# k^T v of the last attention unit ahead of its scores, and the first batch's remainder transposed by DMA

## The chip, the cores and the metric

The kernel runs on one core of one Trainium2 chip. The metric is the device time of one execution in microseconds (us). "The kernel before" is the one that was tuned already, "the changed kernel" the same with the change below. The time of before that the work started from is 535.66 us, the median of three runs.

## The reference

A retention layer feeds a mixture of four experts. Each of 8 batches has 8 heads, 576 tokens and 64 channels per head; all four experts work on every one of the 4608 tokens.

```python
gamma = 1.0 - 2.0 ** (-5.0 - np.arange(H))
Dmat = np.where(rel >= 0, gamma[:, None, None] ** rel[None], 0.0)     # rel = pos_i - pos_j
x = ((q @ k.T) / sqrt(64) * Dmat) @ v                                  # per batch and head
p = domain_probs / (domain_probs.sum(-1, keepdims=True) + 1e-09)
for e in range(4):
    h = np.maximum(x @ w1[e], 0.0)                                     # 512 -> 1024
    out += p[:, e:e + 1] * (h @ w2[e])                                 # 1024 -> 512
```

## The kernel before

The tokens go through the experts in tiles of 512. The first tile starts when the first 512 tokens of batch 0 have passed the retention layer, and its experts run while their weights are still arriving.

Batch 0 is done in four **units** (two halves of tokens times two groups of four heads). A unit has scores (TensorE), a mask with the decays (VectorE), k^T v (TensorE; its copies go to `sbd`, the carried state), and values: the own ones from masked scores and v, and the carried ones from q and `sbd`. The loop over the units, with cuts:

```python
for u in range(NU):
    ...
    us[u].values_own()
    if u + 1 < NU:
        us[u + 1].scores()
    if u == 1:
        us[2].kv(False, us[1].reads)
    us[u].values_carried()
    if u + 2 < NU:
        us[u + 2].trans_pe(1 - u)
    if u in (0, 2):
        us[u + 1].kv()            # the last unit's k^T v: after its scores
    ...
```

The last 64 tokens of a batch are its **remainder**. Its k and q are transposed on TensorE in the kernel before (later batches use `trans_dma`):

```python
def trans_pe(self):
    self.alloc_trans()
    pt = ring_tile("ptr", [128, 2, NP, 128], BF16)
    for i, n, w in ((0, "k", 128), (1, "q", R)):
        for p in range(NP):
            nc.tensor.transpose(pt[:, i, p, 0:w], ...)
    nc.scalar.activation(self.kT, pt[:, 0], Copy)
    nc.scalar.activation(self.qT, pt[:, 1, :, 0:R], Copy)
```

The first tile has 32 **slots**, eight to an expert: four groups of the first layer (`up_group`), then four of the second. Side work is hung on slots. In the first tile the first layer's activation runs on ScalarE:

```python
if t == 0:
    nc.scalar.activation(h[:, fk:fk + 2, :], ph, Relu)
```

and so do the casts of the v inputs of batch 1, which are put into the slots 17, 19, 24 and 25 together with the casts of k and q on VectorE.

```python
def v_cast(u):
    vs[u].cast("k", nc.vector)
    vs[u].cast("q", nc.vector)
    vs[u].cast("v", nc.scalar)      # in line with the activations
    ...
for u, (c, tr, sc, o) in enumerate(((17, 20, 22, 23), (19, 22, 24, 25), (24, 0, 28, 29), (25, 0, 29, 30))):
    add(c, lambda u=u: v_cast(u))
    ...
```

The loads of the first tile are issued in this order on GpSimd's queue: the weights of the second and third expert, q, k and v of batch 1's units 1 and 2, the fourth expert's w1, unit 3, the fourth expert's w2; unit 4's follow once unit 1 is cast.

Of the kernel before, what the change touches and what calls it, by code (L numbers as in the profile page):

```python
# [10 lines left out]
BF16 = mybir.dt.bfloat16  # L11
Copy = mybir.ActivationFunctionType.Copy
# [11 lines left out]
def kernel(  # L24
# [10 lines left out]
    nc = tc.nc  # L35
# [8 lines left out]
    R = S - SM  # L44
    NP = H // 2
# [20 lines left out]
    def ring_tile(name, shape, dt=FP32):  # L66
        return ring.tile(shape, dt, tag="ring", name=name)
# [11 lines left out]
    def load_rem(b, eng=nc.sync):  # L79
        for j in range(2):  # L80
            for n, src in (("k", k), ("v", v)):
                eng.dma_start(out=rawr[n][64 * j:64 * j + 64, :, j, :],
                                  in_=src[b, j:H:2, SM:S, :].rearrange("g t d -> t g d"))
        eng.dma_start(out=rawr["q"][0:R, :, :, :].rearrange("t g j d -> t (g j) d"),
                          in_=q[b, :, SM:S, :].rearrange("h t d -> t h d"))

    rawr = {n: const.tile([128, NP, 2, D], FP32, name=f"rawr_{n}") for n, _ in srcs}
    bfr = {n: const.tile([128, NP, 2, D], BF16, name=f"bfr_{n}") for n, _ in srcs}
# [53 lines left out]
    ident = const.tile([128, 128], BF16)  # L142
# [87 lines left out]
    class Duo:  # L230
# [18 lines left out]
        def kv(self):  # L249
            kvp = ring_tile("kvp", [128, 2, NC, D])  # L250
            for i, p in self.pairs():
                for c in range(NC):
                    for j in range(2):
                        nc.tensor.matmul(kvp[64 * j:64 * j + 64, i, c:NC, :], lhsT=bfs[p % 2]["k"][:, c, j, :],  # L254
                                         rhs=bv[p][:, c, j, :].unsqueeze(1).to_broadcast([128, NC - c, D]),
                                         start=(i == 0 and c == 0), stop=(c == NC - 1), skip_group_check=True)
            for j in range(2):
                r = slice(64 * j, 64 * j + 64)
                nc.scalar.activation(sbd[r, self.ps, :, r], kvp[r], Copy)
# [42 lines left out]
    class Rem:  # L302
# [12 lines left out]
            self.kT = atp.tile([128, NP, 128], BF16, tag="kTr", name="kTr", bufs=1)  # L315
            self.qT = atp.tile([128, NP, R], BF16, tag="qTr", name="qTr", bufs=1)

        def trans_pe(self):
            self.alloc_trans()
            pt = ring_tile("ptr", [128, 2, NP, 128], BF16)  # L320
            for i, n, w in ((0, "k", 128), (1, "q", R)):
                for p in range(NP):
                    nc.tensor.transpose(pt[:, i, p, 0:w], bfr[n][0:w, p, :, :].rearrange("p j d -> p (j d)"),
                                        ident[0:w, 0:w])
            nc.scalar.activation(self.kT, pt[:, 0], Copy)
            nc.scalar.activation(self.qT, pt[:, 1, :, 0:R], Copy)

        def trans_dma(self):
            self.alloc_trans()
            for dst, n, w in ((self.kT, "k", 128), (self.qT, "q", R)):  # L330
                nc.sync.dma_start_transpose(out=dst, in_=bfr[n][0:w, :, :, :].rearrange("p g j d -> p (g j d)"))
# [181 lines left out]
    class Unit:  # L513
# [53 lines left out]
                s[:, :, :, :, :].rearrange("p j g r t -> p (j g) (r t)"),  # L567
                tri0[:, :, :, :].rearrange("p r s t -> p (r s t)").unsqueeze(1).to_broadcast([128, 4, 2 * C]), op=MULT)

        def kv_open(self, u=0):  # L570
            if u == 0:
                self.kvt = ring_tile("kvp0", [128, 2, 2, 2, 128])
            self.kvp = self.kvt[:, u]

        def kv_mm(self, rows, dst, hh, start=False, others=()):
            for g in range(2):
                for r in range(2):
                    two = lambda n: self.bf(n, hh)[0:rows, r, 2 * g:2 * g + 2, :].rearrange("p j d -> p (j d)")
                    rhs = two("v")
                    if dst == slice(0, 2):  # L580
                        rhs = rhs.unsqueeze(1).to_broadcast([rows, 2, 128])
                    mm = nc.tensor.matmul(self.kvp[:, g, dst, :], lhsT=two("k"), rhs=rhs,
                                          start=(start and g == 0 and r == 0), stop=False, skip_group_check=True)
                    for i in others:
                        tc.declare_no_dep(mm.ins, i.ins, reason="another bank of the same tile")
# [4 lines left out]
        def kv(self, fresh=True, others=()):  # L590
            hf, kvp = self.hf, None
            front = hf == 1 and self.carry is None
            if fresh:
                self.kv_open()
                if front:
                    self.kv_front()
            self.kv_mm(128, 1, hf, not front, others)
            self.kv_mm(64, 0, hf, False, others)
            self.reads = []
            kvp = self.kvp  # L600
            gs = slice(2 * self.g, 2 * self.g + 2)
            for j in range(2):
                jr = slice(64 * j, 64 * j + 64)
                dst = sbd[jr, gs, 2 * hf:2 * hf + 2, jr]
                src = kvp[jr, :, :, jr]
                if hf == 1 and self.carry is not None:
                    nc.vector.tensor_tensor(dst, src,
                                            self.carry[jr, gs, :].unsqueeze(2).to_broadcast([64, 2, 2, D]), op=ADD)
                else:
                    self.reads.append(nc.vector.tensor_copy(dst, src) if others else nc.scalar.activation(dst, src, Copy))  # L610
                if hf == 0 and self.carry is not None:
                    nc.vector.tensor_copy(self.carry[jr, gs, :], kvp[jr, :, 1, jr])

# [47 lines left out]
    us = [Unit(0, hf, g, raw0[u], bfv0(g)) for u, (hf, g) in enumerate(units0)]  # L661
# [7 lines left out]
    def cast_unit(u):  # L669
        us[u].cast("k", nc.vector)  # L670
        us[u].cast("q", nc.vector)
        us[u].cast("v", nc.gpsimd)
        for f in load_w1_at.get(u, ()):
            load_w1(0, f)
# [7 lines left out]
    for u in range(NU):  # L682
        if u + 2 < NU:
            cast_unit(u + 2)
        if u == NU - 1:
            part = UpHalf(0)
            part.matmuls(0)
        us[u].values_own()
        if u + 1 < NU:
            us[u + 1].scores()  # L690
        if u == 1:
            us[2].kv(False, us[1].reads)
        us[u].values_carried()
        if u + 2 < NU:
            us[u + 2].trans_pe(1 - u)
        if u in (0, 2):
            us[u + 1].kv()
        if u == 0:
            us[2].kvt = us[1].kvt
            us[2].kv_open(1)  # L700
            us[2].kv_front(us[1].reads)
    part.matmuls(1)
    early.close()
    hp = ctx.enter_context(tc.tile_pool(name="hp", bufs=1))
# [41 lines left out]
    load_v(2)  # L746
    load_w2(3)

    def remainder(slots, b, at):
        add = lambda i, f: slots.setdefault(i, []).append(f)  # L750
        x = Rem(b)
        l, c, tr, s, o = at
        if b > 0:
            add(l, lambda: load_rem(b))
        add(c, lambda: x.cast(nc.vector))
        add(tr, x.trans_pe)
        add(s, x.scores)
        add(o, x.values)

    def run(slots, i):  # L760
        for f in slots.get(i, []):
            f()

    slots = {}
    add = lambda i, f: slots.setdefault(i, []).append(f)
    add(0, later_decays)
    add(3, mixing_weights0)
    add(9, mixing_weights)
    remainder(slots, 0, (-1, 13, 15, 16, 17))

    def v_cast(u):
        vs[u].cast("k", nc.vector)
# [24 lines left out]
    n = 0  # L797
# [18 lines left out]
    slots = {i - 32: f for i, f in slots.items() if i >= 32}  # L816
# [30 lines left out]
    for t in range(1, n_nt):  # L847
        d = [Down(h, t, s) for s in range(2)]
# [5 lines left out]
        n = NS * (t - 1)  # L854
# [40 lines left out]
```

## Time and profile before

| | before |
|---|---|
| median of three runs | 535.66 us |
| profiled span | 534.0 us |
| TensorE busy | 523.8 us (98%) |
| ScalarE busy | 85.3 us (16%) |
| VectorE busy | 362.3 us (68%) |
| first tile on TensorE until the next tile's first matmul | 83.33 us |

TensorE is the bound. Read a gain or a loss from the times at which TensorE starts certain matmuls, and read the reason from the bracket after a line of the timeline: the idle time just before it and what ended it. "DMA" in a slice row or a transfer's landing time tells when its data were there.

### The profile page before, as it was taken

How to read it: one execution, taken by the hardware profiler on the slowest of the kernel's cores; microseconds unless marked ns; L12 is line 12 of the kernel's file. 1: busy time of each engine (PE TensorE's matmuls, PEld its weight loads, DVE VectorE, ACT ScalarE, POOL GpSimd, SP SyncE). 2: the span in 40 equal slices, each digit the busy share in tenths (PEclk: the TensorE clock that was granted, in tenths of full speed). 3: DMA queues.
4: the chain of work that ended last, by engine and by line, in shares of the span. 5: the costliest groups of instructions: out<-in, count | busy, mean ns of one | idle time of the engine just before them, and what ended most of it. 6: DMA issues, size and time to landing. Idle time of an engine off the chain costs nothing.

```text
span 534.0 us, 10194 instructions
## 1 busy us (share of the span) xinstructions
PE 523.8 (98%) x4220; PEld 341.9 (64%) x4259; DVE 362.3 (68%) x458; ACT 85.3 (16%) x173; POOL 147.3 (28%) x191
## 2 busy tenths in 40 slices
PE   8999999999999999999999999999999999999997
PEld 4644544478745885478646865587548844884486
DVE  5435768895577667697578767776765567557763
ACT  4623440012101121020101001100110000000010
POOL 5744104245245334335132614152000000000000
PEclk9999999999999999999999999999999999999999
DMA  9999947777769967946353655454010111110001
GB/s 239 195 212 243 252 129 193 161 155 163 149 168 161 170 133 150 155 84 163 105 135 96 147 137 113 106 115 129 20 41 22 59 39 41 41 41 20 1 24 56
DMA packets 145054, 63.55 MB, mean 119 GB/s; under 512 B 123760, under 2 KB 135808, under 8 KB 145008
## 3 DMA queue, kind: packets, MB, share of 16 engines
q1 hardware_dynamic: 134080, 43.42, 37.3%
q0 software_dynamic: 10784, 19.35, 16.6%
q8 instruction: 33, 0.54, 0.4%
q10 hardware_dynamic: 144, 0.13, 0.1%
q14 instruction: 13, 0.11, 0.1%
HBM read 53.56 MB, written 9.51 MB: 118 GB/s over the span
## 4 chain that ended last, share of the span: by engine, by line
PE 72%; ACT 2%; DMA 1%; issue 0%; DVE 0%; POOL 0%; POOLq 0%
PE ph L358 35%; PE pd L474 34%; ACT xt L291 2%; PE o L283 1%; DMA qTr<-bfr_q 1%; PE o L278 1%; PE py L474 1%; DVE h L364 0%; PE or L343 0%; PE sr L337 0%; PE or L345 0%; POOL bf_k L238 0%; DVE ob L502 0%; PE kvp L254 0%; POOLq L238 0%
## 5 line engine op out<-in xcount | busy, mean ns | idle before, releaser
L358 PE MATMUL ph<-xt,w 128*128 128x512 bf16 x1102 | 249.0, 379 | 2.5 <-DVE h L364 0.2
L364 DVE SCALAR_TENSOR_TENSOR h<-ph,pB 128x1024 bf16<-128x1024 f32 x128 | 156.4, 1223 | 58.7 <-PE ph L358 58.0
L358 PEld LDWEIGHTS <-w 128*128 128x128 bf16 x1136 | 110.0, 98 | 127.8
L474 PEld LDWEIGHTS <-h 128*128 128x128 bf16 x1024 | 100.0, 98 | 13.3
L474 PEld LDWEIGHTS <-s 128*128 128x128 bf16 x768 | 75.0, 98 | 8.7
L474 PE MATMUL pd<-wx,h 128*128 128x256 bf16 x512 | 61.1, 273 | 0.2
L474 PE MATMUL pd<-wx,s 128*128 128x256 bf16 x512 | 61.1, 273 | 0.0
L219 POOL DMA_DIRECT2D pB<-pd x28 | 15.8, 563 | 153.9 <-DVE h L364 153.2
L509 POOL TENSOR_TENSOR ob<-v,p 128x256 f32<-128x256 f32 x15 | 11.3, 754 | 115.0 <-DVE v L506 93.5
L238 POOL TENSOR_TENSOR bf_k<-raw_k,gk 128x512 bf16<-128x512 f32 x24 | 26.4, 1100 | 36.2 <-DMA raw_k<-in_k_dram 22.6
L270 DVE TENSOR_TENSOR sT<-s,tri 128x1024 bf16<-128x1024 f32 x24 | 28.2, 1219 | 6.4 <-PE s L268 6.4
L291 ACT ACTIVATE xt<-o 128x768 bf16<-128x768 f32 (+6 forms) x24 | 13.0, 594 | 116.8 <-PE o L283 116.8
L474 PE MATMUL pd<-t4w,h 128*128 128x256 bf16 x256 | 30.6, 273 | 0.0
L447 DVE TENSOR_TENSOR s<-s,h 128x1024 bf16<-128x1024 bf16 x32 | 30.2, 985 | 0.0
L397 PE MATMUL po<-wx,h 128*128 128x512 bf16 x124 | 28.6, 379 | 0.3 <-issue 0.2
L474 PE MATMUL pd<-t3w,h 128*128 128x256 bf16 x240 | 28.7, 273 | 0.0
L474 PE MATMUL pd<-t2w,s 128*128 128x256 bf16 x240 | 28.6, 273 | 0.0
L482 ACT ACTIVATE p<-pd 128x256 f32<-128x256 f32 x16 | 6.1, 384 | 138.9 <-PE pd L474 112.8
L238 POOL TENSOR_TENSOR bf_q<-raw_q,gq 128x512 bf16<-128x512 f32 x24 | 26.9, 1123 | 2.3 <-DMA rawr_v<-in_v_dram 1.7
L451 DVE TENSOR_TENSOR s<-h,s 128x1024 bf16<-128x1024 bf16 x32 | 25.6, 838 | 0.0
L445 DVE TENSOR_TENSOR s<-h 128x1024 bf16<-128x1024 bf16 x32 | 24.6, 809 | 0.0
L491 DVE TENSOR_TENSOR u<-pd,p 128x256 f32<-128x256 f32 x15 | 6.4, 425 | 22.7 <-PE pd L474 22.6
(161 smaller groups left out, 375.4 us busy)
## 6 DMA issues: line engine op xcount, KB each, us to landing
pB<-pd POOLq DMA_DIRECT2D x28, 256.0 KB, 3.6
raw_k<-in_k_dram SPq DMA_DIRECT2D x48, 128.0 KB, 2.8
raw_q<-in_q_dram SPq DMA_DIRECT2D x48, 128.0 KB, 3.0
raw_v<-in_v_dram SPq DMA_DIRECT2D x48, 128.0 KB, 3.0
out_dram<-oa SPq DMA_DIRECT2D x16, 256.0 KB, 2.2
out_dram<-ob SPq DMA_DIRECT2D x15, 256.0 KB, 2.0
w<-in_moe_w_dram POOLq DMA_DIRECT2D x3, 1024.0 KB, 14.1
wx<-in_moe_w_dram POOLq DMA_DIRECT2D x3, 1024.0 KB, 15.3
```

The source lines that it names most:

```text
L219: eng.dma_start(out=pB[t, e], in_=pd[e:e + 1, t * NT:(t + 1) * NT].to_broadcast([128, NT]))
L238: eng.tensor_tensor(bfs[p % 2][n], raw1[n], g[:, :, 2 * p:2 * p + 2].unsqueeze(3).to_broadcast([128, NC, 2, D]), op=MULT)
L270: nc.vector.tensor_tensor(sT[:, :, :, :].rearrange("p j c t -> p (j c) t"), s[:, :, :, :].rearrange("p j c t -> p (j c) t"), tri[:, :].uns ...
L291: nc.scalar.activation(xt_of(t)[:, self.ps, n0 + a - t * NT:n0 + z - t * NT], o[:, :, a:z], Copy)
L358: nc.tensor.matmul(ph[:, f, :], lhsT=w1_sb[e][:, dc, fc * 128:(fc + 1) * 128], rhs=x[:, dc, :], start=(dc == 0), stop=(dc == NDC - 1))
L364: nc.vector.scalar_tensor_tensor(h[:, fk:fk + 2, :], ph, 0.0, pB[t, e][:, :].unsqueeze(1).to_broadcast([128, 2, NT]), op0=MAX, op1=MULT)
L397: nc.tensor.matmul(po[:, gg, :], lhsT=h[:, e * NFC + fc, (2 * m + gg) * 128:(2 * m + gg + 1) * 128], rhs=wx[e // 2][:, (e % 2) * NFC + fc, ...
L445: nc.vector.tensor_tensor(self.alloc("s1")[:, l], h[:, l, self.b], h[:, r, self.b], op=ADD)
L447: nc.vector.tensor_tensor(self.alloc("s2")[:, l], self.s1[:, l], h[:, l, self.a], op=SUB)
L451: nc.vector.tensor_tensor(self.alloc("s4")[:, l], h[:, r, self.a], self.s2[:, l], op=SUB)
L474: mm = nc.tensor.matmul(dst, lhsT=src[:, kk, tok], rhs=rhs(c), start=(start and c == 0), stop=(c == KH - 1), skip_group_check=True)
L509: nc.gpsimd.tensor_tensor(self.ob[:, HF:Dm], self.v, self.p5, op=ADD)
```

## The change

It has two parts. **Part one** moves the last unit's k^T v ahead of its scores, to fill waits of TensorE at 15 to 17 us; its result goes to a PSUM bank that is free by then. **Part two** takes the eight transposes of batch 0's remainder off TensorE; Sync issues two DMA transposes in slot 11 instead, and the remainder's scores and values move from slots 16 and 17 to 19 and 20, in the third expert. The core of the diff, with cuts:

```diff
         us[u].values_own()
+        if u == 2:
+            us[3].kv(False, us[2].reads)
         if u + 1 < NU:
             us[u + 1].scores()
...
-        if u in (0, 2):
-            us[u + 1].kv()
         if u == 0:
-            us[2].kvt = us[1].kvt
-            us[2].kv_open(1)
+            us[1].kv()
+            us[2].kvp = us[1].kvt[:, 1]
             us[2].kv_front(us[1].reads)
+        if u == 1:
+            us[3].kvp = us[1].kvt[:, 0]
+            us[3].kv_front(us[2].reads)
...
-    remainder(slots, 0, (-1, 13, 15, 16, 17))
+    rem0 = Rem(0)
+    for at, f in ((11, lambda: rem0.cast(nc.vector)), (11, rem0.trans_dma), (19, rem0.scores), (20, rem0.values)):
+        add(at, f)
```

More of the change, by code (lines that the diff above doesn't have):

```diff
@@ L316, in alloc_trans @@
             self.qT = atp.tile([128, NP, R], BF16, tag="qTr", name="qTr", bufs=1)
-        def trans_pe(self):
-            self.alloc_trans()
-            pt = ring_tile("ptr", [128, 2, NP, 128], BF16)
-            for i, n, w in ((0, "k", 128), (1, "q", R)):
-                for p in range(NP):
-                    nc.tensor.transpose(pt[:, i, p, 0:w], bfr[n][0:w, p, :, :].rearrange("p j d -> p (j d)"),
-                                        ident[0:w, 0:w])
-            nc.scalar.activation(self.kT, pt[:, 0], Copy)
-            nc.scalar.activation(self.qT, pt[:, 1, :, 0:R], Copy)
         def trans_dma(self):
@@ L568, in scores @@
                 tri0[:, :, :, :].rearrange("p r s t -> p (r s t)").unsqueeze(1).to_broadcast([128, 4, 2 * C]), op=MULT)
-        def kv_open(self, u=0):
-            if u == 0:
-                self.kvt = ring_tile("kvp0", [128, 2, 2, 2, 128])
-            self.kvp = self.kvt[:, u]
         def kv_mm(self, rows, dst, hh, start=False, others=()):
@@ L593, in kv @@
             if fresh:
-                self.kv_open()
+                self.kvt = ring_tile("kvp0", [128, 2, 2, 2, 128])
+                self.kvp = self.kvt[:, 0]
                 if front:
@@ L609, in kv @@
                 else:
-                    self.reads.append(nc.vector.tensor_copy(dst, src) if others else nc.scalar.activation(dst, src, Copy))
+                    self.reads.append(nc.vector.tensor_copy(dst, src) if not fresh and self.g == 0 else nc.scalar.activation(dst, src, Copy))
                 if hf == 0 and self.carry is not None:
@@ L747 @@
     load_w2(3)
-    def remainder(slots, b, at):
-        add = lambda i, f: slots.setdefault(i, []).append(f)
-        x = Rem(b)
-        l, c, tr, s, o = at
-        if b > 0:
-            add(l, lambda: load_rem(b))
-        add(c, lambda: x.cast(nc.vector))
-        add(tr, x.trans_pe)
-        add(s, x.scores)
-        add(o, x.values)
     def run(slots, i):
```

## The prediction

> **What bounds the kernel now.** I read the page first, then TensorE's timeline where the change acts (13 to 22 us and 46 to 47 us), then VectorE's and ScalarE's timelines beside it, then the DMA views up to 76 us.
>
> ```profile
> span 534.0 us, 10194 instructions
> PE 523.8 (98%) x4220; PEld 341.9 (64%) x4259; DVE 362.3 (68%) x458; ACT 85.3 (16%) x173; POOL 147.3 (28%) x191
> DMA  9999947777769967946353655454010111110001
> ```
>
> TensorE is busy 98% of the span, so its idle time is only 534.0 - 523.8 = 10.2 us, and the change can win by filling idle time or by removing TensorE work. The DMA row says that the engines are full in the first five slices (13.35 us each, to 67 us): while the weights arrive, a transfer added there delays others. Both parts of the change lie in that stretch. Now TensorE around the last attention unit of batch 0 (columns: start us, us, engine, line, operation; in brackets the idle time before and its releaser):
>
> ```profile
> 14.74 0.39 PE L540 MATMUL pt<-ident,bf_q 128*128 128x128 bf16 x4
> 15.66 0.42 PE L625 MATMUL o<-sT,bf_v 64*64 64x128 bf16 x16 [0.53 <-DVE sT L565]
> 16.41 0.42 PE L563 MATMUL s<-qkT 64*64 64x128 bf16 x16 [0.33 <-ACT qkT L542]
> 16.76 0.40 PE L635 MATMUL o<-qkT,sbd 128*128 128x128 bf16 x4
> 16.99 1.15 PE L582 MATMUL kvp<-bf_v,bf_k 128*128 128x256 bf16 x12
> 18.07 1.05 PE L379 MATMUL ph<-xt,w 128*128 128x256 bf16 x8
> 19.05 0.42 PE L625 MATMUL o<-sT,bf_v 64*64 64x128 bf16 x16
> ```
>
> TensorE waits 0.53 us for VectorE's masked scores and 0.33 us for ScalarE's transposed q and k, and the 12 k^T v matmuls of the last unit, which need neither, come after both waits. The rest is the remainder's transposes:
>
> ```profile
> 46.43 0.39 PE L323 MATMUL ptr<-ident,bfr_k 128*128 128x128 bf16 x4
> 46.75 0.29 PE L323 MATMUL ptr<-ident,bfr_q 64*128 64x64 bf16 x4
> 46.97 1.90 PE L358 MATMUL ph<-xt,w 128*128 128x512 bf16 x8
> ```
>
> Eight small transposes hold TensorE from 46.43 to 46.97 us.
>
> **What the Trainium skill says.** First, "PSUM — Partial Sum Buffer", section on PSUM bank collisions: two engines on different banks run clean. The new order needs this, as k^T v of the last unit is written into the first bank of a tile whose second bank VectorE reads at 15.4 to 16.3 us. The kernel before already does the like for the third unit (k^T v at 11.97 us ahead of later reads of the other bank), with right results. Second, "TensorE: Matmul & The Clock Gate", Part 4, gives about 275 ns for one 128x128 transpose in a kernel; the trace has 219 ns each, overlapped, so that eight move the next matmul by 0.54 us, and this is what I use. Third, "DMA: Bandwidth & Descriptors", section on queues and rings: each engine takes its queues in turn, a packet from each. The trace agrees, here from 40 to 41 us, when the small store of the mixing weights shares the engines with the weight loads (packets, MB, share):
>
> ```profile
> q0 software_dynamic: 86, 0.17, 91.8%
> q1 hardware_dynamic: 85, 0.01, 14.6%
> ```
>
> **Part one: k^T v first.** The instruction order says what moves: 4 of the 12 matmuls go between the last q transposes and the values of unit three, 8 between these values and the scores of unit four. The count is the same; only the place is new, and ScalarE's two copies of the result now come before its copies of unit three's output. Step by step, from the timeline:
> - The first four (256 wide, about 0.11 us each as at L379: 8 in 0.98 us) fill about 0.45 of the 0.53 us; the values still start at 15.66 us, when VectorE is done.
> - The eight others take 0.66 us (the same eight for unit three, 13.74 to 14.40 us). They start about 15.98, so the scores start at 16.64 us instead of 16.41: 0.23 us later.
> - Then 0.35 us of scores and 0.23 us of carried values: the expert's first matmuls start at about 17.22 us instead of 18.07, that is 0.85 us earlier.
> - But the values of the last unit need their masked scores. Before, scores at 16.41 gave VectorE's mask from 16.88 to 18.11 us, and nothing waited since TensorE came to the values only at 19.05. Now the mask runs 17.11 to 18.34, and after the 0.15 us that the other units show between mask and values, these start at 18.49, while TensorE is free at 17.22 + 0.98 = 18.20. So 0.29 us of the 0.85 comes back as a new wait.
> Left: 19.05 - 18.49 = **0.56 us**.
>
> **Part two: transposes by DMA.** TensorE loses 8 weight loads and 8 matmuls: **0.54 us**. ScalarE loses two copies (0.60 and 0.38 us) beside the path. VectorE casts the remainder two slots earlier, at about 39 us, in an idle stretch of 7.7 us. The remainder's 4 score and 8 value matmuls are the same, only later: nothing. Sync's queue issues two transposes (about 1.2 us each in the trace) in a stretch where it has nothing else to do until 69 us.
>
> **Sum:** 0.56 + 0.54 = 1.10 us off 535.66, or 534.56 us, if all of it lasts to the end. After 22 us TensorE runs almost without a gap, and what it waits for later (VectorE, ScalarE, GpSimd's casts) follows TensorE's own progress, so an early gain mostly lasts.
>
> **The rivals.**
>
> *The transposes land late and TensorE waits for them.* The inputs of the remainder land at 27.2 + 11.6 = 38.8 us:
>
> ```profile
> rawr_q<-in_q_dram POOLq DMA_DIRECT2D x1, 128.0 KB, 11.6
> pd<-pn SPq DMA_DIRECT2D x1, 72.0 KB, 10.0
> ```
>
> So the transposes are issued between 39 and 42 us, behind the store of the mixing weights, which took 10.0 us for its 512 packets in this traffic. Later transposes on the idle engines show about 512 packets each; the q one here has half the rows, so 768 packets in all. The store's packets are through at about 44 us; packets of this queue pass at up to 147 per us there (42 to 43 us), which gives 5 us more, and about 1 us to the signal: an estimate of 50 us. The scores need them at 54.24 - 0.56 - 0.54 and less 0.34 us of the remainder's own matmuls that stood before: 52.8 us. Slack of some 3 us, on a rough estimate. If they are 2 to 4 us late, the gain is gone and the time is 536 to 538 us. One chance in ten.
>
> *The gain meets a load that does not move.* Weights arrive by the clock of the DMA, not of TensorE. The nearest ones: the second half of the first w2 lands at 15.8 + 10.5 = 26.3 us, and its first matmul, 1.73 us after 25.71, comes forward to 26.9; the second expert's w1 lands at 31.4 for a matmul that moves from 32.62 to 32.06. Both still fit. Worse, the transposes add about 768 packets at some 20 ns each on 16 engines, so about 1 us, to loads that follow. At 69 to 73 us that can bite:
>
> ```profile
> 70.02 0.63 ACT L525 ACTIVATE kv<-raw_v 128x512 bf16<-128x512 f32 x1
> 70.77 1.02 ACT L362 ACTIVATE h<-ph 128x1024 bf16<-128x1024 f32 x1
> 72.49 1.02 ACT L362 ACTIVATE h<-ph 128x1024 bf16<-128x1024 f32 x1 [0.70 <-PE ph L358]
> ```
>
> ScalarE's cast waits for a v load that landed at about 68.9 us; 1 us later it would hold up the two activations behind it, which TensorE needs for the fourth expert's second layer, and cost up to 0.4 us of the 1.1. I give this one chance in two, for about 0.2 us on average.
>
> *The whole 0.85 us of part one stays*, if the mask begins earlier than I reckon; then 534.3 us. One in ten.
>
> **Range and chances.** 534.56 plus 0.15 for the second rival is **534.7 us**. Low end 534.2 (all of part one, nothing lost), high end 535.6 (a short wait for the transposes, or most of the gain lost to loads). TensorE's 523.8 us of work leave no way to 2% (10.7 us) off; 2% slower would need a wait of ten us, which the transposes' slack doesn't suggest. Faster by over 2%: 0.005; within: 0.985; slower: 0.01.
>
> **What would show it.** TensorE's timeline: no idle time over 0.1 us before the values of unit three or the scores of unit four, a new wait of 0.2 to 0.3 us on VectorE before the values of unit four, these at about 18.5 us; no transposes at 46 us, and the third expert's first matmul at about 45.9 us instead of 46.97; the remainder's scores near 52.8 us without a wait on a DMA; TensorE busy 0.5 us less. I am wrong if the remainder's scores wait for the DMA, if the loads after 43 us land over 1 us later and TensorE waits for them, or if the gain at 20 us is not found at the end.

## The result, and the profile after

| | median | range | runs |
|---|---|---|---|
| before | 535.61 us | 535.24 to 535.78 | 6 |
| changed | 535.59 us | 534.99 to 536.02 | 6 |

The ratio is 1.0001, with a 95% interval of 0.9988 to 1.0014: nothing was gained. The forecast, 534.7 us from 535.66, would be a ratio of 0.9982, which lies outside the interval.

The profiled run of the changed kernel was the slowest of its six (536.02 us). Its page, span and busy times:

```profile
span 534.3 us, 10181 instructions
PE 523.6 (98%) x4212; PEld 341.4 (64%) x4251; DVE 362.3 (68%) x458; ACT 84.5 (16%) x171; POOL 148.2 (28%) x191
```

The eight transposes and the two copies are gone (4251 weight loads instead of 4259, 171 ScalarE instructions instead of 173), and the span is no shorter. TensorE's timeline of the changed kernel around the last unit (start us, us, engine, line, operation, in brackets idle time and releaser):

```profile
14.92 0.60 PE L567 MATMUL kvp<-bf_v,bf_k 128*128 128x256 bf16 x4
15.58 0.42 PE L611 MATMUL o<-sT,bf_v 64*64 64x128 bf16 x16
15.93 0.72 PE L567 MATMUL kvp<-bf_v,bf_k 128*128 128x128 bf16 x8
16.59 0.42 PE L553 MATMUL s<-qkT 64*64 64x128 bf16 x16
16.94 0.40 PE L621 MATMUL o<-qkT,sbd 128*128 128x128 bf16 x4
17.17 1.04 PE L369 MATMUL ph<-xt,w 128*128 128x256 bf16 x8
18.34 0.42 PE L611 MATMUL o<-sT,bf_v 64*64 64x128 bf16 x16
```

Part one does what it was meant to do. The two waits of 0.53 and 0.33 us are gone, and the last unit's values start at 18.34 us where before they started at 19.05. Further on in the same timeline:

```profile
22.39 3.40 PE L348 MATMUL ph<-xt,w 128*128 128x512 bf16 x15 [0.69 <-DMA w<-in_moe_w_dram]
...
46.35 7.07 PE L348 MATMUL ph<-xt,w 128*128 128x512 bf16 x32
53.26 0.28 PE L327 MATMUL sr<-qTr,kTr 128*128 128x64 bf16 x4
53.37 1.03 PE L387 MATMUL po<-wx,h 128*128 128x512 bf16 x3
55.30 0.60 PE L387 MATMUL po<-wx,h 128*128 128x512 bf16 x2 [0.91 <-ACT h L352]
56.22 0.60 PE L387 MATMUL po<-wx,h 128*128 128x512 bf16 x2 [0.31 <-ACT h L352]
```

In the kernel before, the two stretches of these waits read:

```profile
22.26 3.62 PE L358 MATMUL ph<-xt,w 128*128 128x512 bf16 x15
54.24 1.89 PE L397 MATMUL po<-wx,h 128*128 128x512 bf16 x8
```

No transposes stand before the third expert any more, and the remainder's scores at 53.26 us wait for nothing. But two new waits have come. At 22.39 us TensorE waits for the last half of the first expert's w1. And the first eight matmuls of the third expert's second layer, which took 1.89 us in one piece in the kernel before (from 54.24 us), now last from 53.37 to 56.22 + 0.60 = 56.82 us, that is 3.45 us, since they wait twice for ScalarE's activations `h`. That hold alone costs 3.45 - 1.89 = 1.56 us. (It is more than the 0.91 + 0.31 us in the brackets, because idle time is counted from the end of a 0.38 us matmul, while the next would have started some 0.22 us after its start.)

Why ScalarE is late is in its own timeline. The kernel before:

```profile
52.07 0.63 ACT L525 ACTIVATE bf_v<-raw_v 128x512 bf16<-128x512 f32 x1
52.71 1.02 ACT L362 ACTIVATE h<-ph 128x1024 bf16<-128x1024 f32 x1
54.44 1.02 ACT L362 ACTIVATE h<-ph 128x1024 bf16<-128x1024 f32 x1 [0.70 <-PE ph L358]
```

and the changed kernel:

```profile
53.70 0.63 ACT L515 ACTIVATE bf_v<-raw_v 128x512 bf16<-128x512 f32 x1 [2.68 <-DMA raw_v<-in_v_dram]
54.24 1.92 ACT L352 ACTIVATE h<-ph 128x1024 bf16<-128x1024 f32 x2
```

Before, the cast of the first v of batch 1 finds its data there, and the second activation waits for TensorE, as it should. After, ScalarE stands 2.68 us before that cast because the load has not landed, and two activations whose inputs are ready run one behind the other only afterwards. The load landed at 52.0 us before and at 53.7 us after. The Trainium skill, "PSUM — Partial Sum Buffer", section "Engine vs sequencer instructions", says that ScalarE's queue is strictly first in, first out; this trace agrees, with two ready activations held until 54.24 us.

To see where the time goes over the whole first tile, take the first starts of marked matmuls from each timeline and their differences (us):

| stretch of TensorE | before | changed | part one only | part two only | changed, all v casts moved |
|---|---|---|---|---|---|
| start to first k^T v | 9.26 | 9.21 | 9.53 | 9.11 | 9.22 |
| to the group of 24 matmuls of the first expert (18.92 us in the changed kernel) | 10.38 | 9.71 | 9.70 | 10.38 | 9.73 |
| to the first expert's second layer | 6.07 | 6.71 | 6.07 | 6.08 | 6.07 |
| to the third expert | 21.26 | 20.72 | 21.26 | 20.72 | 20.72 |
| to the first scores of batch 1 | 12.99 | 14.54 | 12.99 | 13.55 | 12.98 |
| to the fourth expert's second layer | 12.33 | 12.34 | 12.34 | 12.33 | 12.34 |
| to the next tile | 11.04 | 11.04 | 11.04 | 11.05 | 11.04 |
| sum: next tile starts | 83.33 | 84.27 | 82.93 | 83.22 | 82.10 |

In the changed kernel's profile part one gives 0.67 us and part two 0.54 us, just as in the kernels that have only one of them; the weights at 22 us take 0.64 us and the hold in the third expert 1.55 us. With 0.05 us at the start this makes 0.94 us later at the next tile. The profile of before itself lost 0.43 us at 172 us, where it waits for a transpose of a later remainder (0.27 us in the bracket); the changed profile didn't. That is a matter of the draw: the waits there are 0 to 0.85 us in the profiles. From there (172.86 and 173.37 us) to the last group of matmuls both traces take 355.8 us, as do all the others.

So the trace gives the theory: **both parts give what they should, and ScalarE, in line behind a cast whose load comes later, takes it back.** Two rivals: the gain is lost at the first w1, whose arrival doesn't move (0.64 us in this draw); or part two costs more through its traffic than it saves, wherever that is felt.

### The profile page after: what moved, and what is told of

Its sections match the earlier page's. It is cut to its first block, busy times and chain, and to the rows that moved or that the text cites. A ratio compares the mean times of both kernels' runs of the same rounds, so it can differ in the third digit from the quotient of the medians.

```text
span 534.3 us, 10181 instructions
## 1 busy us (share of the span) xinstructions
PE 523.6 (98%) x4212; PEld 341.4 (64%) x4251; DVE 362.3 (68%) x458; ACT 84.5 (16%) x171; POOL 148.2 (28%) x191
## 4 chain that ended last, share of the span: by engine, by line
PE 73%; ACT 2%; issue 0%; DVE 0%
PE ph L348 36%; PE pd L464 34%; ACT xt L291 2%; PE o L283 1%; PE o L278 1%; PE py L464 1%; DVE h L354 0%; PE or L333 0%; PE sr L327 0%; PE or L335 0%; DVE ob L492 0%
## 5 line engine op out<-in xcount | busy, mean ns | idle before, releaser
L464 PEld LDWEIGHTS <-h 128*128 128x128 bf16 x1024 | 100.0, 98 | 13.3
L437 DVE TENSOR_TENSOR s<-s,h 128x1024 bf16<-128x1024 bf16 x32 | 32.4, 1051 | 0.0
L387 PE MATMUL po<-wx,h 128*128 128x512 bf16 x123 | 28.8, 379 | 1.6 <-ACT h L352 1.2
L441 DVE TENSOR_TENSOR s<-h,s 128x1024 bf16<-128x1024 bf16 x32 | 23.4, 772 | 0.0
L387 PEld LDWEIGHTS <-h 128*128 128x128 bf16 x128 | 11.9, 98 | 15.8 <-ACT h L352 2.8
```

What stands on the lines that cost most here:

```text
L387: nc.tensor.matmul(po[:, gg, :], lhsT=h[:, e * NFC + fc, (2 * m + gg) * 128:(2 * m + gg + 1) * 128], rhs=wx[e // 2][:, (e % 2) * NFC + fc, ...
L437: nc.vector.tensor_tensor(self.alloc("s2")[:, l], self.s1[:, l], h[:, l, self.a], op=SUB)
L441: nc.vector.tensor_tensor(self.alloc("s4")[:, l], h[:, r, self.a], self.s2[:, l], op=SUB)
L464: mm = nc.tensor.matmul(dst, lhsT=src[:, kk, tok], rhs=rhs(c), start=(start and c == 0), stop=(c == KH - 1), skip_group_check=True)
```

## The experiments

Each was timed beside the kernel before on the same chip; the medians of before in these sessions were 535.39, 535.56 and 535.50 us (11 runs each). Differences in us below are (ratio - 1) times the median of before. The diffs are shortened: `cast` stands for `lambda: rem0.cast(nc.vector)`, and a quarter or half for a slice of w1's columns.

**Part one alone.** The remainder stays as in the kernel before:

```diff
-    for at, f in ((11, cast), (11, rem0.trans_dma), (19, rem0.scores), (20, rem0.values)):
+    for at, f in ((13, cast), (15, rem0.trans_pe), (16, rem0.scores), (17, rem0.values)):
```

> Part one of the change alone: k^T v of the last unit ahead of its scores; the remainder transposed on TensorE as before. Theory A (the head of the program gains, and what follows loses it only where a load lands late): no transposes on the DMA engines, so the v load of batch 1 lands at about 52 us as in the kernel before and ScalarE's cast of it holds nothing up; the gain at 19 us (0.7 us in the profile of the changed kernel) lasts except where the last part of the first w1 lands late. Time 0.3 to 0.7 us less than before, TensorE's wait for ScalarE's activations at the third expert's second layer under 0.4 us. Rival B (the gain of part one is always lost at 22 us, because w1 lands by the clock of the DMA engines): a wait of 0.6 us or more on w1 before the third pair of first-layer groups, and the time within 0.15 us of before.

Measured: 534.82 us (534.45 to 535.04), ratio 0.9986 (0.9973 to 0.9999), so 0.75 us gained. Part one works by itself and its gain lasts to the end; its stretch in the table is 0.68 us shorter and nothing takes it back. The first v landed at 51.6 us in this profile.

**Part two alone.** The kernel before with:

```diff
-    remainder(slots, 0, (-1, 13, 15, 16, 17))
+    rem0 = Rem(0)
+    for at, f in ((11, cast), (11, rem0.trans_dma), (19, rem0.scores), (20, rem0.values)): add(at, f)
```

> Part two alone: the remainder of batch 0 transposed by DMA, its products in the third expert; the last unit in its old order. Theory A (the added DMA transposes delay the loads behind them by about 1 us, and ScalarE, in order, waits for the v load ahead of two activations that TensorE needs): TensorE waits 0.8 to 1.5 us for activations in the third expert's second layer, which eats the 0.54 us of removed transposes; time from 0 to 0.5 us more than before. Rival C (the transposes cost nothing and all loss is in part one): 0.5 us less than before, and no such wait.

Measured: 535.47 us (535.02 to 535.92), ratio 0.9999 (0.9987 to 1.0011). ScalarE's and TensorE's timelines of this kernel:

```profile
52.66 0.63 ACT L525 ACTIVATE bf_v<-raw_v 128x512 bf16<-128x512 f32 x1 [1.69 <-DMA raw_v<-in_v_dram]
53.19 1.92 ACT L362 ACTIVATE h<-ph 128x1024 bf16<-128x1024 f32 x2
```

```profile
55.17 0.61 PE L397 MATMUL po<-wx,h 128*128 128x512 bf16 x2 [0.31 <-ACT h L362]
```

The 0.54 us are saved (21.26 to 20.72), and 0.56 us are lost in the third expert. So part two alone makes the hold (smaller than the 0.8 to 1.5 us expected): it brings TensorE forward by 0.54 us and the v load came 0.7 us later (52.7 us). Part one adds to the first of these and makes the hold longer. In three profiles with this hold (part two alone, the changed kernel again, below, and the changed kernel) the cast starts at 52.66, 52.96 and 53.70 us, and the first scores of batch 1 come 7.18, 7.18 and 7.19 us later. In these profiles this load sets TensorE's time, and what was gained ahead of it is lost.

**The changed kernel with the first two v casts later.** They are taken out of `v_cast` and hung on slots 20 and 21, behind the third expert's activations (the load of unit 4, which reuses unit 1's buffer, goes with the first):

```diff
-        vs[u].cast("v", nc.scalar)
+        if u > 1:
+            vs[u].cast("v", nc.scalar)
...
+        if u < 2:
+            add(20 + u, lambda u=u: v_cast_v(u))
```

> The changed kernel, but ScalarE's casts of v for the first two units of batch 1 stand behind the activations of the third expert (and behind the copy of the remainder's result) in its order instead of ahead of them. Theory A: the wait of 1.2 us (0.9 and 0.3) for activations at 54 to 56 us goes, nothing takes its place; time 0.8 to 1.2 us less than before. Rival D (the loads are late for everything that follows, so another wait on them replaces it, such as the transposes of these units or the later v casts): time within 0.3 us of before, with a new wait on TensorE between 56 and 80 us.

Measured: 535.41 us (534.82 to 536.3), ratio 0.9996 (0.9984 to 1.0008). The timing alone would be a miss. The profile shows why: the hold in the third expert is gone (12.99 us again), and another one has come in the fourth, in ScalarE's and then TensorE's timeline:

```profile
70.72 0.63 ACT L515 ACTIVATE kv<-raw_v 128x512 bf16<-128x512 f32 x1 [1.46 <-DMA raw_v<-in_v_dram]
71.25 1.92 ACT L352 ACTIVATE h<-ph 128x1024 bf16<-128x1024 f32 x2
```

```profile
73.23 0.61 PE L387 MATMUL po<-wx,h 128*128 128x512 bf16 x2 [0.31 <-ACT h L352]
```

The last v of batch 1 landed at 70.7 us (68.9 before), and the stretch to the next tile is 11.62 instead of 11.04 us. The lateness of the loads has run on to the next cast of the same kind. It is the very place that the prediction named for its second rival.

**The kernel before with two idle DMA transposes.** They write to a buffer that is not used yet, and change nothing else but the slot of the cast:

```diff
+        def idle_trans(self):      # k and q of the remainder into unused columns of t4w
+            ...
+                nc.sync.dma_start_transpose(out=dst, in_=bfr[n][0:w, ...])
-    remainder(slots, 0, (-1, 13, 15, 16, 17))
+    remainder(slots, 0, (-1, 11, 15, 16, 17))      # idle_trans in slot 11
```

> The kernel before with two DMA transposes of the remainder added, into memory that is read by nobody before it is overwritten; its transposes stay on TensorE (its cast two slots earlier, as in the changed kernel). Measures the cost of the added traffic alone. Theory A: the loads issued after 33 us land about 1 us later than in the kernel before (v of batch 1 at about 53 us instead of 52), ScalarE's cast holds its activations, TensorE waits 0.2 to 1 us more; time 0.1 to 0.8 us more than before. Rival E (the later landing in the changed kernel was chance): landings within 0.4 us of before, time within 0.1 us.

Measured: 535.96 us (535.16 to 539.32), ratio 1.0015 (0.9994 to 1.0035), no difference clear of noise. One of the six runs, that of 539.32 us, shows a granted clock of 0.996, the others 0.999 or 1.0. In the profile the first v landed at 54.2 us, and the stretch to the first scores of batch 1 is 13.28 us, 0.29 us longer than before. But this profile also began 0.93 us later on TensorE, so that only part of the later landing is the transposes'. A better measure is within one profile: the time from the landing of the third expert's w1 to that of its w2. It is 5.3 to 5.5 us in the seven profiles without DMA transposes there (before, part one, these two with casts moved, and the three with late transposes, below), and 6.6 to 6.9 us in the seven with them, this one included (44.8 to 51.7). The two transposes delay the loads behind them by some 1.3 us.

**The transposes after the v loads.** The changed kernel with the remainder's cast and transposes in slot 20 and its products in the fourth expert, so that the third expert's loads are not delayed:

```diff
-    for at, f in ((11, cast), (11, rem0.trans_dma), (19, rem0.scores), (20, rem0.values)):
+    for at, f in ((20, cast), (20, rem0.trans_dma), (28, rem0.scores), (29, rem0.values)):
```

> The changed kernel with the remainder's cast and DMA transposes late: about 57 us instead of 39, and its products in the fourth expert. Theory A (in the changed kernel the transposes delay the load stream by 1.0 to 1.4 us just ahead of the loads that ScalarE waits for): wx and v of batch 1 land as in the kernel before, the wait of 1.2 us at 54 to 56 us is gone or under 0.4 us; but the last v load, at 69 us, is now the one that comes about 1 us later, and ScalarE's cast of it may hold TensorE for 0.3 to 0.8 us at 72 us. Time 0.4 to 1.0 us less than before. Rival F (the remainder's move itself costs what it saves): within 0.2 us of the time of part one alone, 0.6 us less than before, without waits.

Measured: 538.94 us (538.05 to 540.07), ratio 1.0063 (1.0051 to 1.0075), **and a wrong result** (relative error 0.163). The mistake is mine: the values of the remainder read the last quarter of `sbd`, the carried state of batch 0, and the last two units of batch 1 write over that quarter in slots 28 and 29. VectorE's first such write starts at 75.5 us, the remainder's values at 79.0 us. The waits of TensorE say it as well (us in total, times, longest):

```profile
PE or L335 <- DVE sbd L593: 2.3, 1, 2.3
```

That is a wait for batch 1's update of the state, which the remainder of batch 0 must not see. So the products have to run before slot 28; the slots 24 to 27 of the fourth expert were not tried. The time says nothing about the change, but the landings do, since they were set before the wrong products ran: with the transposes out of the way, the third expert's w2 landed at 48.9 us and the first v at 51.6 us, no later than in the kernel before (49.4 and 52.0 us). The last v landed at 70.9 us, and its cast held TensorE twice, for 0.54 and 0.31 us, as theory A had it.

**The same with the last v cast later**, in slot 27:

```diff
-        vs[u].cast("v", nc.scalar)
+        if u != 3:
+            vs[u].cast("v", nc.scalar)
...
+        if u == 3:
+            add(27, lambda u=u: v_cast_v(u))
```

> As the run with the late transposes, and ScalarE's cast of the last v of batch 1 behind the two activations that it held. Theory A: no wait for activations over 0.3 us on TensorE up to 83 us; both parts of the change keep what they save: 0.68 + 0.54 us, less 0 to 0.3; time 0.9 to 1.3 us less than before. Rival G (the stream of loads paces TensorE anyway, another load takes over): under 0.6 us less.

Measured: 537.68 us (536.06 to 539.48), ratio 1.0040 (1.0025 to 1.0056), and the same wrong result with the same wait, 2.2 us here. Nothing follows for the change.

**The changed kernel with all three casts later.** The casts of the units 1, 2 and 4 of batch 1 in slots 20, 21 and 27:

```diff
-        vs[u].cast("v", nc.scalar)
+        if u not in {0: 20, 1: 21, 3: 27}:
+            vs[u].cast("v", nc.scalar)
...
+        if u in {0: 20, 1: 21, 3: 27}:
+            add({0: 20, 1: 21, 3: 27}[u], lambda u=u: v_cast_v(u))
```

> The changed kernel with its early DMA transposes, and all of ScalarE's v casts that stood ahead of activations (units one, two and four of batch 1) moved behind them. Theory A: the loads still land 1.0 to 1.5 us late, but nothing in ScalarE's order holds TensorE for them: no wait for activations over 0.3 us; time 0.8 to 1.2 us less than before. Rival G: a wait on another late load replaces it (the v load now needed by k^T v itself), time within 0.4 us of before.

Measured: **534.51 us** (533.78 to 535.87), ratio 0.9982 (0.9970 to 0.9994), so 0.96 us gained. In ScalarE's timeline the activations again wait for TensorE, and the cast comes after them:

```profile
52.85 1.02 ACT L352 ACTIVATE h<-ph 128x1024 bf16<-128x1024 f32 x1 [0.70 <-PE ph L348]
54.93 0.38 ACT L339 ACTIVATE xt<-or 128x256 bf16<-128x256 f32 x1 [1.06 <-PE or L335]
55.21 0.62 ACT L515 ACTIVATE bf_v<-raw_v 128x512 bf16<-128x512 f32 x1
```

The v landed at 52.9 us, no earlier than in the changed kernel run again (below), and it costs nothing now. The next tile starts at 82.10 us, 1.23 us earlier than before, and the last column of the table has both gains and no loss. This kernel beats the kernel before; with the changed kernel it was not timed side by side.

**The last half of the first w1 in two pieces**, the second of them issued one unit later, on top of the last wrong-result kernel:

```diff
-    load_w1_at = {1: (quarter 1,), 2: (quarter 2, half 2)}
+    load_w1_at = {1: (quarter 1,), 2: (quarter 2, quarter 3), 3: (quarter 4,)}
```

> As the late transposes with the last v cast moved, and the last half of the first expert's w1 loaded as two quarters, the second one issued after the cast of the last v of batch 0. The wait of 0.69 us on w1 at 22 us in the profile of the changed kernel came in a draw where that half landed at 22.2 us (20.0 to 21.1 in the draws without a wait). Theory A with this: that wait becomes rarer; time 0 to 0.3 us less than the same kernel without it, highest time of the five lower. Rival: the extra issue on GpSimd delays the loads behind it by 0.7 us, time the same or 0.3 us more.

Measured: 538.13 us (535.92 to 538.99), ratio 1.0043 (1.0028 to 1.0058), wrong result again; nothing follows.

**The kernel before with the same three casts later**, as a control:

```diff
-        vs[u].cast("v", nc.scalar)
+        if u not in {0: 20, 1: 21, 3: 27}:
+            vs[u].cast("v", nc.scalar)
...
+            add({0: 20, 1: 21, 3: 27}[u], lambda u=u: v_cast_v(u))
```

> The kernel before with only the three v casts moved behind the activations in ScalarE's order (a control for the version that gained 1.0 us). Theory A: in the kernel before the casts hold nothing of weight, since TensorE reaches the activations late enough, so the time stays within 0.2 us of before. Rival H (the moved casts are themselves the gain, whatever the change does): 0.5 to 1.0 us less than before.

Measured: 535.94 us (535.17 to 536.31), ratio 1.0003 (0.9991 to 1.0015). Moving the casts gives nothing in a kernel whose loads aren't late. So the 0.96 us above are not a gain of that move; it only keeps what the change gives.

**Part one with the casts later**, the same edit on the first of these kernels:

```diff
-        vs[u].cast("v", nc.scalar)
+        if u not in {0: 20, 1: 21, 3: 27}:
+            vs[u].cast("v", nc.scalar)
...
+            add({0: 20, 1: 21, 3: 27}[u], lambda u=u: v_cast_v(u))
```

> Part one alone, with the v casts moved. Theory A: the transposes' 0.54 us is missing, the rest as in the version with both parts and the casts moved: 0.5 to 0.7 us less than before, so 0.4 to 0.6 us more than that version. Rival I (the DMA transposes are not worth their traffic even with the casts moved): the same time as that version, 1.0 us less than before.

Measured: 534.58 us (534.29 to 535.41), ratio 0.9984 (0.9972 to 0.9996), so 0.86 us. This is the same as with the DMA transposes (0.96 us) within what these runs tell; the two were timed on different chips, each beside the kernel before. The profiles differ, with the next tile at 82.50 us here and 82.10 us there. That the DMA transposes pay once the casts are out of the way is likely by the traces and not shown by the timing.

**The changed kernel again**, without an edit, beside these:

> The changed kernel unaltered, timed beside its variants on one chip, since its own six runs lay in two groups (535.0 to 535.3 and 535.9 to 536.0 us). Theory A: within 0.4 us of before, the runs spread over 1 us, with a wait of 0.5 us or more for activations at the third expert's second layer in the profile. Rival: a gain of 0.5 us or more, its first timing having been an unlucky draw.

Measured: 535.41 us (535.0 to 536.21), ratio 0.9998 (0.9986 to 1.0010). The second draw agrees with the first: no gain. Its profile has no wait for w1 (6.08 us in that stretch) and a shorter hold: the v landed at 52.9 us and the stretch to the first scores of batch 1 is 14.16 us, so 1.17 us were lost. With 0.70 us of part one in this profile and 0.54 us of part two the sum is -0.07 us, against a measured -0.1. The first rival, w1, is therefore not what cancels the gain: it wasn't there in this draw, and the gain was.

**The winner with w1 in quarters**, the edit of the eighth kernel on the seventh:

```diff
+    load_w1_at = {1: (quarter 1,), 2: (quarter 2, quarter 3), 3: (quarter 4,)}
```

> The version with both parts and the v casts moved, and the last half of the first w1 loaded as two quarters. Theory A: the late draws of that half, which cost up to 0.7 us at 22 us, cost less; 0 to 0.3 us less than the version without it (1.0 to 1.4 us less than before), highest of the five runs below 535.3 us. Rival: the extra issue delays later loads, the same or up to 0.3 us more.

Measured: 534.47 us (533.74 to 536.46), ratio 0.9983 (0.9967 to 1.0000). It is no better than without the quarters, and its highest run is not below 535.3 us, as expected, but 536.46. Its profile and that of the winner both have no wait at w1, so the wait seen once at 22 us is a matter of some draws (the half landed at 20.0 to 22.2 us in the profiles), and these runs can't say what it costs on average.

## Why the prediction was right or wrong

The verdict within 2% was right, and the value wrong: 534.7 us was forecast and 535.59 measured. That is the high end of the range (535.6 us), where "most of the gain lost to loads" was put. The working failed at one term, the delayed loads, and at the belief that an early gain lasts.

- **Part one, right.** 0.56 us forecast; the stretch is 0.67 us shorter here and 0.63 to 0.76 us in the other profiles that have it. The new wait for the mask is there, and smaller than reckoned: the values start at 18.34 us instead of 18.49, 0.06 us after the end of the mask and not 0.15 us.
- **Part two's saving, right.** 0.54 us forecast and 0.54 us measured in every profile that has it.
- **The first rival, rightly unlikely.** Landing was estimated at 50 us. Sync's timeline of the changed kernel has the two issues, and the source's view the times from issue to landing:

```profile
39.41 1.33 SPq L321 DMA_TRANSPOSE kTr<-bfr_k  x1
40.83 1.20 SPq L321 DMA_TRANSPOSE qTr<-bfr_q  x1
```

```profile
DMA to landing us min/median/max: 9.1/9.9/10.6
```

So they landed at 39.41 + 9.1 = 48.5 and 40.83 + 10.6 = 51.4 us, and the scores at 53.26 us did not wait. The slack was 1.8 us, not the 3 us of the forecast.
- **The delay of the loads, right in kind and a little small.** About 1 us was forecast, from some 20 ns a packet, and 1.3 us measured. The queues of the changed kernel from 43 to 48 us (packets, MB, share of 16 engines) show the transposes beside the weights:

```profile
q0 software_dynamic: 773, 0.83, 97.0%
q1 hardware_dynamic: 703, 0.16, 28.8%
```

In the same five microseconds the kernel before moved 1.17 MB on the first queue and 0.01 MB on the second. A packet of the second queue took 33 ns here (28.8% of 16 times 5 us, over 703 packets), more than the forecast's 20.
- **The step that failed: the second rival's size and place.** "ScalarE's cast waits for a v load [...] 1 us later it would hold up the two activations behind it [...] cost up to 0.4 us of the 1.1" was the right mechanism. But I looked at 69 to 73 us alone and put it in with 0.2 us. The cast with no slack at all was the first v's: in the kernel before it starts at 52.07 us on a load that landed at 52.0. There both effects meet, a TensorE that comes 0.9 to 1.2 us earlier to the third expert's second layer (53.37 and 53.00 us instead of 54.24) and a load that lands 0.9 to 1.7 us later (it takes 14.3 to 14.4 us from issue to landing instead of 13.1; the rest is when it was issued), and the loss measured is 1.17 and 1.55 us in the two profiles of the changed kernel, and 0.56 us with part two alone. This term is as large as the whole gain. The place that I did look at also costs 0.58 us, once the first is out of the way. The step stands in the prediction as "about 0.2 us on average"; what the runs showed in its place is 0.56 to 1.55 us.
- **"After 22 us TensorE runs almost without a gap ... so an early gain mostly lasts" was false.** Few gaps say that the loads came just in time, not that they came with slack. Of the weights near 22 us I checked two, and not the first w1's last half: it was needed at 22.26 us before, landed at 20.1, and in one draw of the changed kernel at 22.2, where TensorE, then 0.7 us earlier, lost 0.64 us.

What is shown: the hold (by the traces), that it cancels the gain (with the casts moved the change gains 0.96 us, and moving them without the change gives 0), and that part two alone starts it. What stays open: whether part two is worth its transfers once the casts are moved, and what w1's wait costs on average.

## What to carry to other kernels

In this kernel a faster TensorE gained nothing beyond the next load with no slack, so compare landing and first use for every load that follows, not for the nearest few. An instruction that waits for a load should not stand ahead of ready work in an in-order queue; put it where its data have surely arrived. A transfer that frees the busiest engine has its price in what it pushes back in the queues (here 1.3 us), and here another consumer of the loads paid it.

## What the Trainium skill lacked or had wrong

- "DMA: Bandwidth & Descriptors", section "Rules for kernel authors", says that a transpose next to ordinary DMAs needs nothing. That is about right results, and the runs agree. What it costs the ordinary DMAs beside it is on no page: two transposes of 0.20 MB in all (128 x 512 and 64 x 512 values of 2 bytes) put the loads behind them back by some 1.3 us.
- "TensorE: Matmul & The Clock Gate", Part 4, gives the time of one transpose. What a row of them costs the next matmul is missing: eight small ones cost 0.54 us in every pair of profiles here, 68 ns each.
- No page that I read gives the spread of landings from one execution to the next. The last half of the first w1 landed at 20.0 to 22.2 us in these profiles, from the same place in the program. In the new order, where TensorE wants it at 21.4 to 22.0 us, the landing at 22.2 us made it wait; those up to 21.1 us did not.
